# Identity products in TensorE's waits of the first ten slots, and six units of weights moved to later slots

## The chip, the cores and the metric

The kernel runs on one core of a Trainium2 chip. The time is device microseconds of one launch; each kernel is run several times and the median is given. The engines are named as in the profile: TensorE (PE; its weight loads are PEld), VectorE (DVE), ScalarE (ACT), GpSimd (POOL) and SyncE (SP), which issues most of the DMAs. A slot, a word that comes back all through this text, is one turn of the kernel's main loop.

## What is computed

Top-32 attention for 8 batches and 8 heads (576 rows, 64 columns a head), then a bridge to 4608 tokens of 512 features, then a two-layer network with the exact Gelu:

```python
def _attn_ref(q, k, v):
    scores = scale * np.matmul(q, k.transpose(0, 1, 3, 2))
    kth = np.partition(scores, -top_k, axis=-1)[..., -top_k:-top_k + 1]
    scores = np.where(scores >= kth, scores, -1000000000.0)
    attn = np.exp(scores - np.max(scores, axis=-1, keepdims=True))
    attn = attn / (np.sum(attn, axis=-1, keepdims=True) + 1e-09)
    return np.matmul(attn, v).astype(np.float32)
...
    x = np.ascontiguousarray(attn_out.transpose(0, 2, 1, 3)).reshape(B * S, H * D)
    h = x @ w_in
    g = 0.5 * h * (1.0 + erf(h * inv_sqrt2))
    return (g @ w_out).astype(np.float32)
```

q, k and v are float32. The weights w_in (512 x 2048) and w_out (2048 x 512) come as float64, so the kernel turns them into float32 itself.

## The kernel before

An item is 128 query rows of a pair of heads; there are 144 items, 18 for each batch. The main loop runs slots n = 0 to 147, and every engine's instructions stand in the order in which the loop writes them. Slot n does, for different items, all steps of the pipeline:

- TensorE: the scores of item n+2 (t_ps L283 and s_ps L287, or L303 and L314 for the items of the last 64 rows), the product with V of item n-3 where a pair of row blocks is complete (o, L466 or L477; the code calls this `product`), and the transposes of item n-2: the tail (tp_t, L411 or L416), then twice four blocks (tp, L429). In some slots it also transposes parts of q and k of a pair to come (tp_qk, L242; `prep`).
- ScalarE: copies of the scores (L297, L298), two softmax passes of item n-1 (L379 with Prelu, L380 with Exp, once for each head), the copies of the transposed blocks out of PSUM (pt, L412 and L436; qk, L246) and of the product with V into xT (L471, `copy_x`), and Gelu (L529, with its table load).
- VectorE: the top 32 of item n in four rounds (MAX8 L340, MATCH_REPLACE8 L343) for two heads, then the reciprocal of item n-1 (L366).
- GpSimd: thresholds (L355, L358), the denominator (den, L372), and the normalising of item n-1 (L392, two instructions). In slots ahead of some units of weights the normalising is on VectorE instead.

PSUM tiles with the tag tp (transposes, t_ps, o) share two buffers, so a transpose waits until the tile two before it has been copied out.

**The network's pieces.** x @ w_in and g @ w_out are cut into pieces of about 0.9 us on TensorE (`l1_piece`, h_ps L518; `l2_piece`, y_ps L554). `mlp(1)` puts the next piece into the slot, if its tokens are there. The first 256 tokens are complete in slot 10, which the code calls START (2 * NP + 2). Slots 10 and 11 take four pieces each (`left`), later ones eight. What the attention part leaves over is done after the last item.

**Units of weights.** The weights come in 16 units, one a slot, in the order ORDER. A unit takes the low and high words of float64 numbers through one staging tile: `load_weights` issues two DMAs of half a MB in all on SP (L160), `weights_size` is two or three instructions on ScalarE (L175, L177, and L179 where GpSimd doesn't do it), `weights_add` is one addition on GpSimd (L194), preceded by L191 where the unit is "on pool", and a second addition is L206. `SLOT_OF` says which slot a unit is in: before, the places 0 to 14 of ORDER are in slots 1 to 15 and the last is in slot 17. The unit of slot n+1 is sized at the end of slot n and added at the start of slot n+1; the unit of slot n+2 is loaded at the end of slot n. Units in slots up to START get their second addition late in the slot (`ends_late`); units from slot 12 on are "on pool".

The staging tile is a free part of w_out_sb (two halves, taken in turn) for most places of ORDER, and a tile of its own, `words`, with one buffer, for the places 12, 14 and 15, because by then w_out_sb is filling up. A load into a staging tile waits until the unit that was there before has been added.

**Warming up.** Before the loop, nine products of a tile of zeros (L630) run on TensorE while the first DMAs land.

Of the kernel before, what the change touches and what calls it, by code (L numbers as in the profile page):

```python
# [14 lines left out]
def kernel(  # L15
# [19 lines left out]
    nc = tc.nc  # L35
    f32, i32, u32 = mybir.dt.float32, mybir.dt.int32, mybir.dt.uint32
# [5 lines left out]
    P = 128  # L42
# [19 lines left out]
    ps = ctx.enter_context(tc.tile_pool(name="ps", bufs=2, space=bass.MemoryType.PSUM))  # L62
    ctx.enter_context(tc.manual_schedule())

    ident = const.tile([P, P], f32, name="ident")
# [18 lines left out]
    def load(n, pair, queue=None, queue2=None):  # L84
        if pair >= n_pairs:
            return
        queue = queue or nc.sync
        queue2 = queue2 or queue
        b, h0 = pair // NP, 2 * (pair % NP)
        t, src = raw_of(n, pair), sources[n]  # L90
        for e in range(2):
            queue.dma_start(
                out=t[:, 0:NM, e, :], in_=src[b, h0 + e, 0:SM].rearrange("(t p) d -> p t d", p=P)
            )
            queue2.dma_start(out=t[e * TL : (e + 1) * TL, NM, e, :], in_=src[b, h0 + e, SM:S])
# [14 lines left out]
    UNITS = NWI + FT // 2  # L110
# [3 lines left out]
    def weights_of(u):  # L114

        if u < NWI:
            c, r = u // 2 * WS, u % 2 * 2
            return w_in, r, c, w_in_sb[:, r : r + 2, c : c + WS]
        r = 2 * (u - NWI)
        return w_out, r, 0, w_out_sb[:, r : r + 2, :]  # L120


    ORDER = [0, 1, 2, 3, 8, 9, 4, 5, 10, 11, 6, 7, 12, 13, 14, 15]
    FIRST = 1
    START = 2 * NP + 2
    WARM = 9
    words = {}
# [3 lines left out]
    nc.gpsimd.memset(high, EXP0 * 2.0**-21)  # L131


    SLOT_OF = {u: FIRST + i + (i == UNITS - 1) for i, u in enumerate(ORDER)}
    UNIT_IN = {n: u for u, n in SLOT_OF.items()}
    unit_in = UNIT_IN.get

    def load_weights(n, queue=None):

        queue = queue or nc.sync  # L140
        u = unit_in(n)
        if u is None:
            return
        src, r, c, dst = weights_of(u)
        if src.dtype == f32:
            for x in range(2):
                queue.dma_start(
                    out=dst[:, x], in_=src[(r + x) * P : (r + x + 1) * P, c : c + WS]
                )
            return  # L150


        half, i = src.bitcast(u16), ORDER.index(u)
        if i not in (12, 14, 15):
            at = FT // 2 + 4 * (i % 2)
            t = w_out_sb[:, at : at + 4, :].rearrange("p (a b) n -> p a (b n)", a=2)
        else:
            t = stage.tile([P, 2, 2 * WS], f32, tag="words", name="words")
        for a in range(2):
            queue.dma_start(  # L160
                out=t[:, a].bitcast(u16)[:, 0 : 4 * WS - 1],
                in_=half[(r + a) * P : (r + a + 1) * P, 4 * c + 1 : 4 * (c + WS)],
            )
        words[u] = t

    def parts(u):

        t, dst = words[u], weights_of(u)[3].bitcast(i32)
        return t[:, :, 0::2], t.bitcast(mybir.dt.int16)[:, :, 2::4], t[:, :, 1::2].bitcast(i32), dst

    def weights_size(u):
        if u not in words:
            return
        w, first, below, d = parts(u)
        nc.scalar.activation(d, first, func=AF.Relu, bias=low, scale=2.0**19)  # L175

        nc.scalar.activation(below, first, func=AF.Prelu, bias=high, scale=2.0**-21, alpha=2.0**40)  # L177
        if not on_pool(u):
            nc.scalar.activation(w.bitcast(i32), w.bitcast(u32), func=AF.Copy, scale=2.0**-13)  # L179

    def on_pool(u):

        return u in words and SLOT_OF[u] >= START + 2

    made = set()

    def weights_add(u):
        if u in words:
            w, _, below, d = parts(u)
            if on_pool(u):  # L190
                nc.gpsimd.tensor_scalar(  # L191
                    w.bitcast(i32), w.bitcast(u32), 2.0**-13, None, op0=ALU.mult
                )
            nc.gpsimd.tensor_tensor(d, d, below, op=ALU.add)  # L194
            if not ends_late(u):
                weights_end(u)
        made.add(u)

    def ends_late(u):

        return u in words and SLOT_OF[u] <= START

    def weights_end(u):
        if u in words:
            w, _, _, d = parts(u)
            nc.gpsimd.tensor_tensor(d, d, w.bitcast(i32), op=ALU.add)  # L206
# [143 lines left out]
    def threshold(i):  # L350

        if i < 0 or i >= N:
            return
        st = stat_of[i]
        nc.gpsimd.tensor_scalar(  # L355
            st["neg"], st["top"][:, :, 0 :: TOPK - 1], -1.0, None, op0=ALU.mult
        )
        nc.gpsimd.tensor_tensor(  # L358
            st["bias"], st["neg"][:, :, 0], st["neg"][:, :, 1], op=ALU.subtract
        )  # L360

    def inverse(i):
        if i < 0 or i >= N:
            return
        st = stat_of[i]
        nc.vector.reciprocal(st["rden"], st["den"])  # L366

    def add_small(i):
        if i < 0 or i >= N:
            return  # L370
        st = stat_of[i]
        nc.gpsimd.tensor_scalar(st["den"], st["den"], 1e-9, None, op0=ALU.add)  # L372

    def softmax(i, e):

        if i < 0 or i >= N:
            return
        st, s = stat_of[i], row(i, e)
        nc.scalar.activation(s, s, func=AF.Prelu, bias=st["neg"][:, e, 1:2], scale=1.0, alpha=STEEP)  # L379
        nc.scalar.activation(  # L380
            s, s, func=AF.Exp, bias=st["bias"][:, e : e + 1], scale=1.0,
            accum_out=st["den"][:, e : e + 1],
        )
# [56 lines left out]
    def copy_x():  # L440
        while copies:
            copies.pop()()
# [149 lines left out]
    def run_gelus():  # L592
        while waiting:
            gelus(waiting.pop(0))
# [9 lines left out]
    def mlp(n):  # L604
        for _ in range(n):
            if done[0] >= len(pieces) or pieces[done[0]][0] > ready[0] or left[0] == 0:
                return
            pieces[done[0]][1]()
            done[0] += 1
            left[0] -= 1  # L610
            if eager[0]:
                run_gelus()
# [7 lines left out]

    load("k", 1)
    load("q", 1)
    for n in range(2):
        load_weights(FIRST + n)


    idle = raws["v"][0][:, NM].rearrange("p e d -> p (e d)")
    warm = ps.tile([P, 512], f32, tag="l1", name="warm")
    for _ in range(WARM):
        nc.tensor.matmul(warm[:, 0:P], lhsT=idle, rhs=idle, start=True, stop=True)  # L630
    for pair in range(2):
        for piece in transpose_qk(pair, pair == 0):
            piece()
# [17 lines left out]
    for n in range(ahead):  # L651

        left[0] = 4 if n in (START, START + 1) else 8
        eager[0] = n > N
        weights_add(unit_in(n))
        scores(n + 2)
        product = attend(n - 3)
        late = n > START
        if n <= START:

            softmax(n - 1, 0)
        copy_x()
        mlp(1)
        tr = transposes(n - 2)
        if product and n > START and done[0] < len(pieces) and pieces[done[0]][0] > ready[0]:

            for piece in tr[:1]:
                piece()
            tr, ready[0] = tr[1:], n_tok[0]
        if n > START:  # L670
            softmax(n - 1, 0)
        mlp(1)
        if not late:
            softmax(n - 1, 1)
        mlp(1)
        prep = prep_in.pop(n, [])
        if len(prep) > 1 and len(tr) == 3:
            tr, prep = tr[:1] + prep[:1] + tr[1:], prep[1:]
        for piece in tr[:-1]:
            piece()  # L680
            ready[0] = n_tok[0]
            mlp(1)
        ready[0] = n_tok[0]
        if late:
            softmax(n - 1, 1)
        add_small(n - 1)
        if ends_late(unit_in(n)):
            weights_end(unit_in(n))
        for piece in tr[-1:] + prep:
            piece()  # L690
            mlp(1)

        run_gelus()
        mlp(left[0])
        run_gelus()
        if n < N:
            top_k(n, {3: lambda: inverse(n - 1)})
        else:
            inverse(n - 1)
        threshold(n)  # L700
        u = unit_in(n + 1)

        normalise(n - 1, 2 if on_pool(u) else 0)

        weights_size(unit_in(n + 1))
        if n >= FIRST:
            load_weights(n + 2)
        if n <= NP:
            load("v", n)

# [37 lines left out]
```

## Time and profile before

| | |
|---|---|
| median of 5 runs | 1640.95 us (1640.01 to 1642.09) |
| the profiled execution | 1640.01 us, of which its span (first to last instruction) is 1638.2 us |
| mean granted TensorE clock | 0.981 of full speed |
| TensorE busy | 1586.8 us, 97% of the span |
| VectorE busy | 1415.0 us, 86% |
| ScalarE busy | 1185.8 us, 72% |
| GpSimd busy | 663.0 us, 40% |
| chain that ended last | TensorE 92%, ScalarE 5%, all others 1% or less each |

The span differs from the time by what lies before the first and after the last instruction, 1.8 us here. In the page's second part the span is cut into 40 slices of 41 us, and each digit is the busy share of an engine in tenths; PEclk is the TensorE clock that the throttle granted. A list of waits names the waiting instruction, what it waited for by its line, the total in microseconds, how often, and the longest. In a timeline a row is: start, duration, engine, line, operation, output and inputs, how many instructions are merged in it, and in brackets the idle time of the engine just before and what ended it. One f32 product is two records on TensorE, one transpose is one.

A table of windows shows how full the engines are at the start: between 20 and 120 us VectorE is busy for every microsecond, ScalarE for 18.0 to 18.7 of each 20, GpSimd for 14.5 to 18.5 of each 20 and TensorE for 9.8 to 15.0, at a mean granted clock of 0.60 to 0.79. From 140 to 1600 us TensorE is busy at the full clock almost without a gap.

### The profile page before, as it was taken

What the parts mean: (1) busy time and instruction counts of PE and PEld (TensorE: products, weight loads), DVE (VectorE), ACT (ScalarE), POOL (GpSimd) and SP (SyncE); (2) the same over time, 40 slices, a digit from 0 to 9 for tenths busy, and PEclk for the clock granted to TensorE, in tenths of its full rate; (3) what the DMA queues carried; (4) which work ended last, traced back from release to release, by engine and by line L of the source; (5) the groups of instructions that cost most, each with busy time, mean ns of one, the idle gap of its engine ahead of it and who ended that gap; (6) DMA issues with size and microseconds to landing.
All of it is one profiled execution on the core that took longest, in us unless ns stands there. A gap on an engine that the chain in (4) does not pass through costs nothing.

```text
span 1638.2 us, 25030 instructions
## 1 busy us (share of the span) xinstructions
PE 1586.8 (97%) x8818; PEld 1075.2 (66%) x8818; DVE 1415.0 (86%) x3046; ACT 1185.8 (72%) x2133; POOL 663.0 (40%) x759
## 2 busy tenths in 40 slices
PE   5579999999999999999999999999999999999999
PEld 4356676766666666676666667676666666666665
DVE  8999999988898899998989898998889889999800
ACT  6999877777777777777777777777777777777720
POOL 4897533333333333333333333333333333333300
PEclk7779999999999999999999999999999999999999
DMA  6433210011101120001110111001110101000000
GB/s 165 143 110 121 55 43 1 14 33 40 35 1 28 30 51 8 14 16 36 30 28 15 28 30 43 1 14 32 41 36 1 28 16 35 1 14 3 5 13 13
DMA packets 126765, 56.14 MB, mean 34 GB/s; under 512 B 117776, under 2 KB 118064, under 8 KB 126640
## 3 DMA queue, kind: packets, MB, share of 16 engines
q1 hardware_dynamic: 125376, 54.12, 12.3%
q8 instruction: 70, 1.15, 0.3%
q10 hardware_dynamic: 1200, 0.39, 0.1%
q14 instruction: 55, 0.45, 0.1%
q0 software_dynamic: 64, 0.03, 0.0%
HBM read 45.08 MB, written 9.44 MB: 33 GB/s over the span
## 4 chain that ended last, share of the span: by engine, by line
PE 92%; ACT 5%; POOL 1%; issue 1%; DVE 1%; DMA 1%; SPq 0%; ACTq 0%; POOLq 0%; DVEq 0%
PE y_ps L554 30%; PE h_ps L518 30%; PE o L466 9%; PE tp L429 8%; PE s_ps L287 8%; PE tp_qk L242 2%; PE t_ps L283 2%; PE o L477 1%; ACT s L380 1%; PE s_ps L314 1%; PE tp_t L411 1%; ACT s L379 1%; POOL s L392 1%; ACT w_in_sb L175 1%; ACT s L297 1%
## 5 line engine op out<-in xcount | busy, mean ns | idle before, releaser
L340 DVE MAX8 top<-rest 128x8 f32<-128x576 f32 x864 | 609.2, 746 | 0.0
L518 PE MATMUL h_ps<-xT,w_in_sb 128*128 128x256 f32 (+1 forms) x2560 | 553.0, 361 | 0.0
L554 PE MATMUL y_ps<-w_out_sb,g 128*128 128x512 f32 x1152 | 548.9, 599 | 0.0
L392 POOL TENSOR_SCALAR s<-s,rden 128x576 f32<-128x576 f32 x278 | 476.9, 1725 | 0.6 <-DVE rden L366 0.4
L518 PEld LDWEIGHTS h_ps<-xT,w_in_sb 128*128 128x128 f32 x2560 | 428.4, 191 | 61.8 <-issue 16.8
L343 DVE MATCH_REPLACE8 rest<-top,rest 128x576 f32<-128x576 f32 x576 | 423.2, 742 | 0.0
L372 POOL TENSOR_SCALAR den<-den 128x2 f32<-128x2 f32 x144 | 32.0, 222 | 836.2 <-ACT s L380 835.8
L554 PEld LDWEIGHTS y_ps<-w_out_sb,g 128*128 128x128 f32 x1152 | 195.1, 190 | 168.2 <-issue 167.3
L297 ACT ACTIVATE s<-s_ps 128x1024 f32<-128x1024 f32 x127 | 130.5, 1028 | 164.5 <-PE s_ps L287 142.2
L380 ACT ACTIVATE s<-s,bias 128x576 f32<-128x576 f32 x288 | 223.3, 775 | 13.2 <-ACT s L379 0.7
L379 ACT ACTIVATE s<-s,neg 128x576 f32<-128x576 f32 x288 | 224.1, 778 | 0.3 <-POOL neg L355 0.2
L436 ACT COPY pt<-tp 128x512 f32<-128x512 f32 x256 | 147.3, 575 | 101.6 <-PE tp L429 101.6
L429 PEld LDWEIGHTS tp<-ident,s 128*128 128x128 f32 x1152 | 145.6, 144 | 100.8 <-issue 58.9
L343 DVE MATCH_REPLACE8 rest<-top,s 128x576 f32<-128x576 f32 x288 | 211.7, 743 | 0.0
L340 DVE MAX8 top<-s 128x8 f32<-128x576 f32 x288 | 201.7, 742 | 1.4 <-ACT s L293 1.4
L429 PE MATMUL tp<-ident,s 128*128 128x128 f32 x1152 | 178.0, 278 | 14.1 <-ACT pt L412 11.6
L466 PE MATMUL o<-pt,raw_v 128*64 128x256 f32 x1280 | 155.8, 391 | 0.0
L287 PE MATMUL s_ps<-qk 64*128 64x256 f32 x1024 | 151.5, 416 | 0.8 <-ACT s L295 0.8
L366 DVE RECIPROCAL rden<-den 128x2 f32<-128x2 f32 x144 | 23.1, 160 | 137.7 <-POOL den L372 137.4
L466 PEld LDWEIGHTS o<-pt,raw_v 128*64 128x64 f32 x1280 | 87.8, 139 | 66.6 <-issue 22.8
L287 PEld LDWEIGHTS s_ps<-qk 64*128 64x128 f32 x1024 | 91.3, 193 | 23.4 <-issue 1.3
L529 ACT ACTIVATE g<-h_ps 128x512 f32<-128x512 f32 x144 | 78.6, 595 | 37.8 <-PE h_ps L518 37.1
(71 smaller groups left out, 1075.2 us busy)
## 6 DMA issues: line engine op xcount, KB each, us to landing
raw_q<-in_q_dram SPq DMA_DIRECT2D x64, 128.0 KB, 2.4
raw_v<-in_v_dram SPq DMA_DIRECT2D x64, 128.0 KB, 2.5
w_out_sb<-in_moe_w_in_dram SPq DMA_DIRECT2D x16, 511.8 KB, 4.9
raw_k<-in_k_dram SPq DMA_DIRECT2D x62, 128.0 KB, 2.5
out_dram<-y SPq DMA_DIRECT2D x31, 256.0 KB, 2.2
w_out_sb<-in_moe_w_out_dram SPq DMA_DIRECT2D x10, 511.8 KB, 3.9
words<-in_moe_w_out_dram SPq DMA_DIRECT2D x6, 511.8 KB, 4.5
out_dram<-y SPq DMA_DIRECT2D x9, 128.0 KB, 2.3
```

The costliest lines, as they stand in the source:

```text
L287: nc.tensor.matmul(s_ps[:, e, c * 256 : (c + 1) * 256], lhsT=lhsT[rows, :], rhs=qk[rows, KT + c * 256 : KT + (c + 1) * 256], start=True, s ...
L297: nc.scalar.activation(spread(s, S + TL, SM), s_ps, func=AF.Copy, scale=scale)
L340: nc.vector.max(st["top"][:, e, 8 * r : 8 * r + 8], cur[e])
L343: nc.vector.match_replace(rest[:, e], st["top"][:, e, 8 * r : 8 * r + 8], cur[e], LOWEST)
L379: nc.scalar.activation(s, s, func=AF.Prelu, bias=st["neg"][:, e, 1:2], scale=1.0, alpha=STEEP)
L380: nc.scalar.activation(s, s, func=AF.Exp, bias=st["bias"][:, e : e + 1], scale=1.0, accum_out=st["den"][:, e : e + 1],)
L392: (nc.vector if e >= 2 - on_dve else nc.gpsimd).tensor_scalar(s, s, st["rden"][:, e : e + 1], None, op0=ALU.mult)
L429: nc.tensor.transpose(tp[:, j * P : (j + 1) * P], s[:, first + j * P : first + (j + 1) * P], ident)
L436: nc.scalar.copy(out=dst, in_=tp.rearrange("p (j n) -> p j n", j=NM))
L466: nc.tensor.matmul(o[e * D : (e + 1) * D, 0:n], lhsT=vt[:, j, e, :], rhs=pt[:, e * NM + j if j < NM else 2 * NM, :], start=(j == 0), stop= ...
L518: nc.tensor.matmul(h_tile(u)[:, i, :], lhsT=w_in_sb[:, ko, f * P : (f + 1) * P], rhs=xT[:, ko, c0 : c0 + n], start=(ko == 0), stop=(ko == ...
L554: nc.tensor.matmul(y_of[sub], lhsT=g_of[u][:, i, sub * P : (sub + 1) * P], rhs=w_out_sb[:, f, :], start=(f == 0), stop=(f == FT - 1),)
```

## The change

It has two parts.

First, products of the identity matrix. The warm-up loop becomes a function, `keep_busy(count, m)`, which still runs the nine products of zeros at the start. In slots 0 to 9 it is called again with the identity: after the second softmax pass has been written and ahead of the transposes (4 products in slot 0 and in slots with a product with V, 14 in the others), between the tail's transpose and the first four blocks in the slots with a product with V (5), and at the end of slot 1 (8). From slot 5 on the first two numbers are doubled. In all there are 183 such products: 4, 22, 14, 14, 9, 28, 18, 28, 18, 28 in slots 0 to 9. Their result is never read.

Second, the slots of the units. The places 0 to 9 of ORDER stay in slots 1 to 10; the six others go to slots 13 to 18 in place of 11 to 15 and 17. Slots 11 and 12 have no unit, slots 16 and 18 get one. The last unit (slot 18) is handled apart (`waits`): it is loaded at the end of slot 17 and not of slot 16, and sized and added within slot 18, behind `copy_x`. The unit at place 2 of ORDER (slot 3) is staged in `words`. "On pool" now means every unit after START, six in place of five.

```diff
-    FIRST = 1
...
-    SLOT_OF = {u: FIRST + i + (i == UNITS - 1) for i, u in enumerate(ORDER)}
+    SLOT_OF = dict(zip(ORDER, [*range(1, START + 1), *range(START + 3, START + 9)]))
...
-        if i not in (12, 14, 15):
+        if i not in (2, 12, 14, 15):
...
-        return u in words and SLOT_OF[u] >= START + 2
+        return u in words and SLOT_OF[u] > START
+
+    def waits(u):
+
+        return u == ORDER[-1]
...
-    warm = ps.tile([P, 512], f32, tag="l1", name="warm")
-    for _ in range(WARM):
-        nc.tensor.matmul(warm[:, 0:P], lhsT=idle, rhs=idle, start=True, stop=True)
+    def keep_busy(count, m):
+        warm = ps.tile([P, 512], f32, tag="l1", name="warm")
+        for _ in range(count):
+            nc.tensor.matmul(warm[:, 0:P], lhsT=m, rhs=m, start=True, stop=True)
+
+    keep_busy(WARM, idle)
...
-        weights_add(unit_in(n))
+        if not waits(unit_in(n)):
+            weights_add(unit_in(n))
...
         copy_x()
+        if waits(unit_in(n)):
+            weights_size(unit_in(n))
+            weights_add(unit_in(n))
...
+        if n < START:
+
+            keep_busy((4 if product or n == 0 else 14) * (1 if n < 5 else 2), ident)
...
             piece()
+            if n < START and product and piece is tr[0]:
+                keep_busy(5 if n < 5 else 10, ident)
...
+        if n == 1:
+            keep_busy(8, ident)
...
-        weights_size(unit_in(n + 1))
-        if n >= FIRST:
-            load_weights(n + 2)
+        if not waits(unit_in(n + 1)):
+            weights_size(unit_in(n + 1))
+        for m in (n + 1, n + 2):
+
+            if m > 2 and waits(unit_in(m)) == (m == n + 1):
+                load_weights(m)
```

More of the change, by code (lines that the diff above doesn't have):

```diff
@@ L622 @@
     load("q", 1)
-    for n in range(2):
-        load_weights(FIRST + n)
+    for n in range(1, 3):
+        load_weights(n)
     idle = raws["v"][0][:, NM].rearrange("p e d -> p (e d)")
-    warm = ps.tile([P, 512], f32, tag="l1", name="warm")
-    for _ in range(WARM):
-        nc.tensor.matmul(warm[:, 0:P], lhsT=idle, rhs=idle, start=True, stop=True)
+    def keep_busy(count, m):
[3 more added lines that the diff above has]
+    keep_busy(WARM, idle)
     for pair in range(2):
```

## The prediction

> **What bounds the kernel now.** I read the slices of the page first, then TensorE's waits by stretch, then two-microsecond windows around the turn, then the timeline of ScalarE and TensorE there.
>
> ```profile
> PE   5579999999999999999999999999999999999999
> DVE  8999999988898899998989898998889889999800
> ACT  6999877777777777777777777777777777777720
> PEclk7779999999999999999999999999999999999999
> ```
>
> Each digit is 41 us. In the first three slices VectorE is full, TensorE is half busy and its granted clock is low; after that TensorE is full to the end. So the end is (the moment from which TensorE never waits) + (the work it then has). VectorE takes 9.70 us a slot (its reciprocals L366 stand at 88.05, 97.75, 107.45 and 117.15) and has no idle time in the ten slots before the turn. Nothing that happens on TensorE before slot 10 is worth anything unless it moves that turn.
>
> ```profile
> PE tp_t L411 <- POOL s L392: 3.7, 1, 3.7
> PE tp L429 <- ACT pt L412: 2.4, 2, 1.8
> PE t_ps L283 <- ACT pt L436: 1.6, 2, 1.4
> ...
> PE tp L429 <- ACT pt L412: 0.8, 1, 0.8
> PE tp_t L416 <- POOL s L392: 0.7, 1, 0.7
> ...
> PE tp_t L416 <- POOL s L392: 0.7, 1, 0.7
> ```
>
> TensorE's waits (us, times, longest) in 100 to 135, 135 to 200 and 200 to 1570 us. All that can still be won behind the turn is here: from 114 us on 0.64 + 1.39 (slot 11), 0.79 (slot 12), 0.72 (slot 18) and 0.7 near the end.
>
> ```profile
> 104.00:106.00 2.00, 0.26 (x2) 0.00 (x0) 2.00 (x6) 1.97 (x7) 1.30 (x2) 0.50 0.00 0
> ...
> 110.00:112.00 2.00, 2.00 (x12) 0.85 (x10) 2.00 (x5) 2.00 (x3) 2.00 (x2) 0.50 0.86 256
> ...
> 114.00:116.00 2.00, 2.00 (x14) 1.80 (x13) 2.00 (x6) 1.97 (x7) 0.92 (x1) 1.00 0.02 4
> ```
>
> Columns: PE, PEld, DVE, ACT, POOL busy, granted clock, DMA. TensorE enters slot 10 at half clock and has the full one from about 113. But ScalarE is full too:
>
> ```profile
> 107.21 0.59 ACT L436 COPY pt<-tp 128x512 f32<-128x512 f32 x1 [0.72 <-PE tp L429]
> ...
> 116.94 0.59 ACT L436 COPY pt<-tp 128x512 f32<-128x512 f32 x1 [0.26 <-PE tp L429]
> ...
> 127.72 0.49 PE L283 MATMUL t_ps<-qk 128*128 128x128 f32 x2 [1.39 <-ACT pt L436]
> ...
> 137.43 0.66 PE L429 MATMUL tp<-ident,s 128*128 128x128 f32 x4 [0.79 <-ACT pt L412]
> ```
>
> ScalarE waits for TensorE once a slot, for the second four transposes: 0.72 us where the clock is halved (four take 1.11), 0.26 where it is full (0.66). TensorE's waits behind the turn are waits for ScalarE's queue, in which 3.5 us of weights (L175, L177, L179) stand in slot 11 and 2.4 in slot 12.
>
> **Part 1, the identity products (183 of them).** Slots 0 to 4 get 4, 22, 14, 14, 9; slots 5 to 9 get 28, 18, 28, 18, 28. Price of one: no row shows it. Lower end: four transposes at full clock, each with its own weight load, pass in 0.44 us (135.18 to the next at 135.62), 0.11 a record; a product has two records, so 0.22. The nine products of zeros at the start agree: 18 records in 4.2 us, 0.23 a record, at a halved clock (the transposes at 5.11 still take 1.08 for four, at 6.98 only 0.66). Upper end: one 128-column product t_ps keeps TensorE from 118.90 to 119.22, 0.32. I take 0.22, a stream of equal records.
>
> [...]
>
> Do they hold the clock? The waits after which it falls are 3.66 (slot 9) and 4.15 to 4.50 (slots 5, 7); across 1.34 and 1.07 (slot 6) it stays at 1.0. Slot 9: scores end at 99.2, 28 x 0.22 = 6.2 fill up to 105.4, so the wait of 3.66 is gone. They write to the l1 buffers, which nothing reads before slot 10.
>
> What it is worth: not the shorter o products (3.43 to 2.38), because behind them TensorE waits in slot 10 for ScalarE: the second transposes at 116.24 wait for a copy behind the softmax, which ends at 115.94 on a queue that was full. So the gain is ScalarE's lead. Waits of 0.72 stand in slots 2, 3, 5, 7 and 9; each becomes 0.26: 5 x 0.46 = 2.3. Two caps. Slot 8: its first four transposes come after ten products, which come after the tail, which needs VectorE's end of slot 7 (88.05) + threshold 0.5 + two L392 of 1.72 = 92.0; + 0.1 + 10 x 0.22 + 0.6 = 94.9, against the copy at 96.24 now: a lead of 1.3 at most. Slot 9: from t_ps (97.72) 0.32 + 1.06 + 6.16 + 0.11 + 0.6 = 8.25 against 8.19 now (copy at 105.91): -0.1, then + 0.46. Lead at the turn: 1.3 - 0.1 + 0.46 = 1.7. Its ends: 0 if a product costs 0.235, 2.3 if the caps don't bind.
>
> **Part 2, six units later.** Slots 11 and 12 lose theirs, 16 and 18 gain one; 13, 14, 15 and 17 keep one. The unit that was in slot 11 had three ScalarE instructions, now two; GpSimd does the third (L191, 3.13), so GpSimd gains 3.1 and ScalarE loses 1.1 us, both beside a full TensorE. Normalising on VectorE (two of 0.52) leaves slot 11 and enters the end of slot 15, before a reciprocal that waits 2.01 for den: covered.
>
> Slot 11: without weights ScalarE takes the scores when they are there, 120.35 instead of 122.20, but then waits for TensorE: its first four transposes end at 124.55 as before. Then copy 0.5, softmax 1.6, copy 0.5: t_ps of slot 12 at 127.27, not 127.72: 0.45 won, and 1.4 us of waiting stay. Slot 12: scores copied 2.9 us after t_ps, not 5.1; the tail's copy is 2 us earlier and the 0.79 goes.
>
> Slot 16 is the price. There ScalarE starts with a table load and Gelu, now followed by L175 and L177 (2.43 at 185.59 to 188.02). Gelu ends at 175.5; weights to 177.95; scores, xT, first softmax pass, table, Exp: the tail's copy ends at 182.5, and the transposes due at 181.87 need its buffer: 0.63 lost. In slot 14, the same shape, Gelu ran 0.9 earlier against t_ps and TensorE didn't wait. Behind it nothing more is late: the last copy of the slot ends at 186.2, t_ps is due at 186.5.
>
> Slot 18: the unit is sized behind copy_x in its own slot, so its wait for the DMA stands ahead of the tail's copies and the softmax on ScalarE. GpSimd is done with the words buffer in slot 17 at 194.05 + 0.63; issue and 4.5 us to landing (3.6 to 6.8 seen for this tile) give 199.8, ScalarE comes there at 199.9; two activations to 202.4, tail copies to 203.0, and the transposes need them at 203.7. Taken at 0; at 6.8 it costs 1.5. SP's queue behind this load holds V loads that now issue at 209.95. The last unit isn't in words when slot 17 normalises, so that stays on GpSimd, and so does the 0.72. GpSimd then ends the unit at 208.4; its first use is slot 19's fifth piece, after 213.
>
> The words buffer for slot 3's unit takes a wait from SP's queue that was 0.1 us (30.92, issued right behind K at 30.30): nothing.
>
> **Sum.** 1.7 + 0.45 + 0.79 - 0.63 = 2.3 us. The profiled execution had a span of 1638.2 in 1640.01; it becomes 1635.9 in 1637.7. The median of the runs is 0.94 above it: 1638.6. Own range 1637.0 to 1640.2 (lead 0.5 to 2.5, slot 16 at 0 to 1).
>
> **Rivals.**
> - All waits go (chance 0.20). TensorE runs on from slot 10: 1.7 + 0.64 + 1.39 + 0.79 + 0.72 = 5.2, so 1635.7 (1634.8 to 1637.2). For it: ScalarE loses 6 us of work in slots 11 and 12. Against: in slot 11 the softmax can't start before TensorE's transposes.
> - The lead is given back (0.17). At 0.235 a product slots 5 to 9 lose 120 x 0.015 = 1.8: 1640.4 (1639.5 to 1643, with slot 18 late). For it: 8.25 against 8.19 in slot 9.
> - Slower: the products are too long (0.13). At 0.32 each odd slot's chain grows by 28 x 0.10 = 2.8 three times, each even one by 1.8 less its 0.5 of slack twice: 11.0 later, less five waits of 0.46, less 0.6 from part 2: 8.1, so 1649. VectorE would not notice (the scores copied at 101.48 are wanted at 117.2), but TensorE and ScalarE would enter slot 10 late and never catch up. Decides from 0.265 (5.6 us lost over 120 products). Against: the transposes' 0.11 a record.
>
> Forecast 0.50. A difference under 0.2% (3.3 us) can't be told from none here: faster means under 1637.7. That is 0.12 of the forecast and the first rival, 0.32; slower 0.13; the rest 0.55. The range 1635.2 to 1642.0 leaves out the slow rival and the edges of two others, 0.18.
>
> **What would show it.** Right: granted clock 1.0 in every window from 40 to 120 us; ScalarE's wait before L436 0.26 in slots 5, 7 and 9; products 0.22 apart; t_ps of slot 12 near 125.6; a wait near 0.6 in slot 16 and none in slot 12. Wrong: products 0.25 apart or more, first transposes of slots 5, 7, 9 later than now, a wait for DMA on ScalarE in slot 18, or VectorE idle before slot 11.

## The result, and the profile after

The changed kernel takes 1638.75 us (median of 25 runs, 1637.57 to 1644.4); the kernel before, run on the same chips, 1640.93 (45 runs, 1639.82 to 1642.7). The ratio is 0.9989, 95% interval 0.9983 to 0.9994. The forecast was 1638.6 us. The gain can be measured, but at 0.11% to 0.13% it lies below the 0.2% from which the prediction calls a kernel faster.

The profiled execution took 1637.79 us, with a span of 1636.0. Lines of the kernel that stood at L283 or behind it are four higher now: t_ps is L287, s_ps L291, the transposes tp L433, the tail tp_t L415 or L420, the normalising L396. The slices of the page and the chain that ended last:

```profile
PE   7999999999999999999999999999999999999999
DVE  8999999988898899998989899998889889999800
ACT  6989877777777777777777777777777777777720
PEclk9999999999999999999999999999999999999999
...
PE 91%; DVE 5%; ACT 2%; POOL 1%; issue 0%; SPq 0%; DMA 0%; DVEq 0%; POOLq 0%; ACTq 0%
```

TensorE is now full, and at nine tenths of its clock or more, in the second and third slices too, from 41 to 123 us. The work that fills them has no use of its own: TensorE's busy time rose by 26.3 us (1586.8 to 1613.1), the time fell by 2. The chain tells more: before, ScalarE had 5% of it, now VectorE has. The early part of this chain now runs through the engine that was full there all along. TensorE's waits in 100 to 135 and 135 to 200 us. From 200 us on there is none, and there was none before either: the 0.7 that the prediction reads as "near the end" is slot 18's wait once more, as its transpose runs from 199.94 us across the border at 200. It stands in none of the prediction's sums.

```profile
PE t_ps L287 <- ACT pt L440: 1.8, 2, 1.4
PE tp_t L415 <- POOL s L396: 1.3, 1, 1.3
PE tp L433 <- ACT pt L416: 0.4, 2, 0.2
...
PE tp_t L420 <- POOL s L396: 0.7, 1, 0.7
PE tp L433 <- ACT pt L416: 0.5, 1, 0.5
```

The 3.7 of slot 9 and the 0.8 of slot 12 are gone. The 1.4 of slot 11 and the 0.7 of slot 18 stand as forecast. A 1.3 in slot 10 is new (TensorE is early there and waits until GpSimd has normalised the tail), and so is the 0.5 of slot 16. The windows around the turn, and three earlier ones:

```profile
38.00:40.00 2.00, 1.95 (x8) 1.41 (x10) 2.00 (x5) 1.93 (x3) 2.00 (x2) 0.67 0.03 8
40.00:42.00 2.00, 2.00 (x10) 1.27 (x7) 2.00 (x6) 1.99 (x2) 1.92 (x3) 0.50 0.51 111
50.00:52.00 2.00, 2.00 (x12) 0.94 (x10) 2.00 (x6) 2.00 (x3) 2.00 (x2) 0.50 0.58 133
104.00:106.00 2.00, 1.66 (x13) 1.11 (x11) 2.00 (x6) 1.74 (x5) 1.16 (x3) 1.00 0.00 0
110.00:112.00 2.00, 0.66 (x5) 0.51 (x4) 2.00 (x5) 1.91 (x4) 2.00 (x2) 1.00 0.00 0
```

At 104 and 110 us, where the clock was 0.50, it is 1.00. But at 40 and 50 us it is still 0.50 (0.86 on average from 40 to 60 us): the sign "1.0 in every window from 40 to 120 us" did not come for slots 3 and 4, and the experiments come back to that. TensorE's timeline:

```profile
92.02 0.33 PE L415 MATMUL tp_t<-ident,s 128*128 128x128 f32 x1 [0.67 <-POOL s L396]
92.19 2.40 PE L636 MATMUL warm<-ident 128*128 128x128 f32 x20
94.42 1.04 PE L433 MATMUL tp<-ident,s 128*128 128x128 f32 x8
...
97.67 6.52 PE L636 MATMUL warm<-ident 128*128 128x128 f32 x56
104.02 0.27 PE L415 MATMUL tp_t<-ident,s 128*128 128x128 f32 x1
...
125.77 0.49 PE L287 MATMUL t_ps<-qk 128*128 128x128 f32 x2 [1.39 <-ACT pt L440]
...
179.56 0.66 PE L433 MATMUL tp<-ident,s 128*128 128x128 f32 x4 [0.49 <-ACT pt L416]
```

Slot 9's 28 products pass from 97.67 to the tail at 104.02, 0.227 us each. ScalarE's side of it:

```profile
95.06 1.07 ACT L440 COPY pt<-tp 128x512 f32<-128x512 f32 x2 [0.82 <-PE tp L433]
...
105.62 0.59 ACT L440 COPY pt<-tp 128x512 f32<-128x512 f32 x1 [0.26 <-PE tp L433]
...
115.43 0.59 ACT L440 COPY pt<-tp 128x512 f32<-128x512 f32 x1 [0.26 <-PE tp L433]
```

The second copies of slots 9 and 10 (105.62, 115.43) wait 0.26, where the clock is full, not 0.72; in slots 5 to 8 the two copies stand in one row, with no such wait between them. Slot 8's first copy waits for TensorE at 95.06: the cap that the prediction put at 94.9.

Where the 2.2 us of span came from can be read off the starts of t_ps, the first product of a slot, before minus after: 1.59 in slot 10, 1.50 in slot 11, 1.95 in slot 12, 2.96 in slots 13 to 16, 2.25 from slot 17 on, and nothing more happens to the end. So the gain at the turn (the point from which TensorE hardly waits any more) is 1.50, slot 11 brings 0.45, slot 12 brings 1.01, slot 16 takes 0.71. Of the 1.50, 0.17 is no work of the change: VectorE itself had started that much earlier in this execution (its reciprocal of slot 9 at 107.28, before at 107.45).

### The profile page after: what moved, and what is told of

Read it like the earlier page. It is cut to its first block, busy times and chain, and to the rows that moved or that the text cites. A ratio compares the mean times of both kernels' runs of the same rounds, so it can differ in the third digit from the quotient of the medians.

```text
span 1636.0 us, 25758 instructions
## 1 busy us (share of the span) xinstructions
PE 1613.1 (99%) x9184; PEld 1106.8 (68%) x9184; DVE 1414.8 (86%) x3046; ACT 1186.1 (73%) x2132; POOL 665.9 (41%) x760
## 4 chain that ended last, share of the span: by engine, by line
PE 91%; DVE 5%; ACT 2%; POOL 1%; issue 0%; SPq 0%; DMA 0%; DVEq 0%; POOLq 0%; ACTq 0%
PE h_ps L522 30%; PE y_ps L558 30%; PE o L470 8%; PE s_ps L291 7%; PE tp L433 7%; DVE top L344 3%; DVE rest L347 2%; PE tp_qk L246 2%; PE t_ps L287 2%; PE o L481 1%; PE tp_t L415 1%; PE s_ps L318 1%; POOL s L396 1%; ACT s L384 0%; ACT s L383 0%
## 5 line engine op out<-in xcount | busy, mean ns | idle before, releaser
L396 POOL TENSOR_SCALAR s<-s,rden 128x576 f32<-128x576 f32 x278 | 476.8, 1725 | 0.6 <-DVE rden L370 0.4
L433 PEld LDWEIGHTS tp<-ident,s 128*128 128x128 f32 x1152 | 142.5, 141 | 88.9 <-issue 58.9
L433 PE MATMUL tp<-ident,s 128*128 128x128 f32 x1152 | 172.8, 273 | 3.7 <-ACT pt L416 3.3
L291 PE MATMUL s_ps<-qk 64*128 64x256 f32 x1024 | 147.1, 406 | 0.8 <-ACT s L299 0.8
L291 PEld LDWEIGHTS s_ps<-qk 64*128 64x128 f32 x1024 | 89.1, 188 | 22.4 <-ACT s L299 1.0
```

The source lines that it names most:

```text
L291: nc.tensor.matmul(s_ps[:, e, c * 256 : (c + 1) * 256], lhsT=lhsT[rows, :], rhs=qk[rows, KT + c * 256 : KT + (c + 1) * 256], start=True, s ...
L396: (nc.vector if e >= 2 - on_dve else nc.gpsimd).tensor_scalar(s, s, st["rden"][:, e : e + 1], None, op0=ALU.mult)
L433: nc.tensor.transpose(tp[:, j * P : (j + 1) * P], s[:, first + j * P : first + (j + 1) * P], ident)
```

## The experiments

Times are medians with the lowest and highest run, and the ratio is to the kernel before, timed beside them on the same chip (medians 1640.64 to 1641.22). Every trace is that of one execution. Diffs are against the changed kernel where nothing else is said.

### Each part alone

The products without the moved units: the slots, the staging and the order of the units as before. This diff is against the kernel before; `keep_busy` itself is left out of it.

```diff
+        if n < START:
+
+            keep_busy((4 if product or n == 0 else 14) * (1 if n < 5 else 2), ident)
...
+            if n < START and product and piece is tr[0]:
+                keep_busy(5 if n < 5 else 10, ident)
...
+        if n == 1:
+            keep_busy(8, ident)
```

> The identity products alone, with the units in their old slots. Theory (the terms add): ScalarE's lead of 1.5 us at the turn is kept through slots 11 and 12, whose waits of 0.64, 1.39 and 0.79 stay, and slot 16 has no wait: 1640.95 - 1.5 = 1639.4. Rival (the lead is worth something only because slots 11 and 12 are free of weights): the weights of slot 11 swallow it and the time is 1640.9.

The moved units without the products:

```diff
-        if n < START:
-
-            keep_busy((4 if product or n == 0 else 14) * (1 if n < 5 else 2), ident)
...
-            if n < START and product and piece is tr[0]:
-                keep_busy(5 if n < 5 else 10, ident)
...
-        if n == 1:
-            keep_busy(8, ident)
```

> The moved units alone, without any identity product. Theory: 0.45 won in slot 11, 0.8 to 1.0 in slot 12, 0.5 lost in slot 16, so about 0.95 in all: 1640.0, with ScalarE's waits of 0.72 still in slots 5, 7 and 9 and the clock at 0.5 there. Rival (the later units stall slots 16 and 18 for more than they free): 1641.5 or more.

Measured: the products alone 1639.24 (1638.67 to 1639.79, 11 runs; ratio 0.9990, 0.9981 to 0.9999), the slots alone 1640.31 (1639.75 to 1641.56, 11 runs; 0.9998, 0.9989 to 1.0007). Against 1640.83 that is 1.6 and 0.5, 2.1 together, where the whole change brings 2.2: the parts add up. The second can't be told from zero by its interval, but its trace can tell: t_ps takes 8.37 us from slot 11 to slot 12 as in the changed kernel (8.82 before), 12.01 over slot 12 (13.02 before) and 13.19 over slot 16 (12.46 before), 0.7 in all. The span of that execution is only 0.2 us shorter than before, because it came to slot 11 0.53 late (119.43 against 118.90), as it had to slot 10 (108.37 against 107.85). Its mean clock from 20 to 40 us was 0.50, before 0.60; that the half microsecond comes from there is the author's estimate and not shown.

The trace of the products alone also shows what a short wait really costs. TensorE in slot 12, first the products alone, where the 0.8 is still there, then the changed kernel:

```profile
134.29 1.03 PE L518 MATMUL h_ps<-xT,w_in_sb 128*128 128x256 f32 x4
136.10 0.65 PE L429 MATMUL tp<-ident,s 128*128 128x128 f32 x4 [0.78 <-ACT pt L412]
136.60 1.03 PE L518 MATMUL h_ps<-xT,w_in_sb 128*128 128x256 f32 x4
```

```profile
133.66 1.03 PE L522 MATMUL h_ps<-xT,w_in_sb 128*128 128x256 f32 x4
134.53 0.60 PE L433 MATMUL tp<-ident,s 128*128 128x128 f32 x4
134.97 1.03 PE L522 MATMUL h_ps<-xT,w_in_sb 128*128 128x256 f32 x4
```

From one h_ps to the next (134.29 to 136.60, 133.66 to 134.97) it is 2.31 against 1.31, so the wait in brackets, 0.78, costs 1.00. In an unbroken stream h_ps takes 0.87 to the next row, though its own row says 1.03: the ends overlap. A wait takes this overlap (0.16) as well, and the transposes behind it take 0.50 to the next row and not 0.44. That makes 0.22 more than the bracket says.

### The unit that moved into slot 16

```diff
-    SLOT_OF = dict(zip(ORDER, [*range(1, START + 1), *range(START + 3, START + 9)]))
+    SLOT_OF = dict(zip(ORDER, [*range(1, START + 1), *range(START + 2, START + 6), START + 7, START + 8]))
```

The six units are in slots 12, 13, 14, 15, 17 and 18, none in slot 16.

> The change with the six units in slots 12, 13, 14, 15, 17 and 18, so none in slot 16. Theory: the 0.49 of slot 16 comes back, but slot 12's wait for the second transposes returns with 1.0, as Gelu, its table loads and the weights stand there together too: 0.5 slower than the change, 1639.3. Rival (slot 12's old wait came from slot 11's weights alone, so slot 12 has room): 0.49 faster, 1638.3.

Measured 1639.54 (1637.81 to 1643.68, 11 runs; 0.9992, 0.9984 to 1.0001). The wait of slot 16 is gone, and the 0.8 of slot 12 is back: a unit in slot 12 makes ScalarE late there again, as in the kernel before. Slot 16 is the cheaper of the two by 0.3 (1.01 against 0.71), in the direction of the medians, which differ by less than these runs spread, so the times alone decide nothing here. The rest of the 0.9 by which this execution's span is longer than the changed kernel's is a smaller lead at slot 10, which the account of the lead below takes up.

### The products that are too many, or not needed

Eight more in each of slots 5, 7 and 9:

```diff
-            keep_busy((4 if product or n == 0 else 14) * (1 if n < 5 else 2), ident)
+            keep_busy((4 if product or n == 0 else 14) * (1 if n < 5 else 2)
+                      + (8 if n >= 5 and not product else 0), ident)
```

> The change with 36 products in slots 5, 7 and 9 instead of 28. Theory (TensorE's chain from t_ps to the first transposes is as long as ScalarE's slot, so each product more is paid): 8 x 0.22 = 1.76 more in each odd slot, so 1.3 of lead lost in each net of the 0.46 won; lead -3.0 instead of 1.5, time 4.5 above the change: 1643.2. Rival (VectorE and GpSimd set the pace of these slots and the products only fill waits): 1638.8, as the change.

Measured 1643.7 (1643.1 to 1644.92, 10 runs; 1.0017, 1.0008 to 1.0026), 5.0 above the changed kernel; its theory said 4.5. TensorE in slot 9:

```profile
101.43 8.30 PE L636 MATMUL warm<-ident 128*128 128x128 f32 x72
109.57 0.27 PE L415 MATMUL tp_t<-ident,s 128*128 128x128 f32 x1
...
111.53 0.49 PE L287 MATMUL t_ps<-qk 128*128 128x128 f32 x2
```

The tail passes 5.55 us later than in the changed kernel (104.02). Of this, 1.06 was there when slot 5's products began (59.99 against 58.93); then each eight products add 1.79, 0.22 each, in slots 5, 7 and 9 alike, and slots 6 and 8 give back 0.31 and 0.58. So nothing of them is hidden in their own slots: 28 is the whole of the room, as the prediction said (8.25 of work against 8.19), and as slot 9 of the changed kernel shows as well, where ScalarE takes the first transposes (104.13 to 104.73) at 104.78 without a wait. This is the mechanism of its slower rival, with that rival's 0.5 of slack in the even slots. Only VectorE did notice: in this trace it is busy for 19.84, 19.24 and 18.34 of each 20 us from 60 to 120, in the changed kernel for all of them.

The count not doubled in slots 5 to 9:

```diff
-            keep_busy((4 if product or n == 0 else 14) * (1 if n < 5 else 2), ident)
+            keep_busy((4 if product or n == 0 else 14), ident)
...
-                keep_busy(5 if n < 5 else 10, ident)
+                keep_busy(5, ident)
```

> The change with the numbers of slots 0 to 4 in slots 5 to 9 too: 14 in odd slots, 4 and 5 in even ones. Theory: the gap that is left in odd slots is 2.4 to 2.8 us, less than the 3.66 across which the clock fell before, so the clock holds; the cap of slot 8 (products behind the tail) is lifted by 1.1 and slot 9's chain is short, so the lead becomes 2.2 and the time 0.7 below the change: 1638.05. Rival (the clock falls in such gaps): waits of 0.72 back in slots 5, 7, 9, lead 0.5 at most, 1639.8.

Measured 1638.82 (1637.34 to 1639.51, 11 runs; 0.9986, 0.9977 to 0.9995), between its theory and its rival. The theory's clock did not hold: it fell with half the products, to 0.91, 0.91 and 0.70 in 60 to 80, 80 to 100 and 100 to 110 us, and slot 9's second copy waited 0.72 again. t_ps of slot 10 starts at 106.59, 0.33 later than in the changed kernel, yet the median is the changed kernel's within its spread: the doubling is worth a few tenths at most, and these runs don't say more.

None in slots 0 to 4:

```diff
-        if n < START:
+        if 5 <= n < START:
...
-            if n < START and product and piece is tr[0]:
+            if 5 <= n < START and product and piece is tr[0]:
...
-        if n == 1:
-            keep_busy(8, ident)
```

> The change without the 63 products of slots 0 to 4. Theory: the lead comes from slots 5, 7 and 9 alone, 3 x 0.46 less 0.1 = 1.3 instead of the 1.5 of the change, so the time is 0.2 above the change's 1638.75: 1638.95. Rival (the early products hold the clock for slot 5; without them its 28 products run at half clock, 12 us instead of 6): lead gone, 1642 or more.

Measured 1639.3 (11 runs; 0.9995, 0.9986 to 1.0004), in two heaps: six runs from 1638.65 to 1639.3, five from 1640.93 to 1641.69. The median is the top of the lower heap, which lies where the theory put the time; the upper heap lies a little below the rival's 1642. But the rival's mechanism is not what happened: in the profiled execution, which is of the upper heap (1641.5), slot 5's 28 products passed at full clock, from 61.41 us on (1.00 in 60 to 80 us). TensorE's row and VectorE's, from the two timelines:

```profile
52.98 4.24 PE L470 MATMUL o<-pt,raw_v 128*64 128x256 f32 x20
```

```profile
59.58 0.17 DVE L370 RECIPROCAL rden<-den 128x2 f32<-128x2 f32 x1 [0.59 <-POOL den L376]
```

The product with V of slot 4 falls into a stretch at half clock (4.24; 3.38 before), and VectorE, which has no wait in these slots in the changed kernel, waits 0.59 us for a denominator. Its reciprocals were 0.14 behind the changed kernel's until then (49.21 against 49.07) and are 0.8 behind from there on (69.30 against 68.47, 108.11 against 107.28). TensorE's lead is gone too: t_ps of slot 10 comes 0.31 after VectorE's reciprocal (before 0.40 after it, in the changed kernel 1.02 ahead of it). Together that is 2.1 us at slot 11. The other 1.64 of this execution's loss is a lower clock in slot 12 (scores in 1.98 and product with V in 3.17, at full clock 1.13 and 2.38), far behind slots 0 to 4; all_filled shows the same fall below, and what brings it on stays open.

### The lead, and what caps it

The lead is how much earlier than before ScalarE, and with it t_ps of slot 10, comes to the turn. The prediction's first cap on it is slot 8: first the tail, then ten products, then the transposes. Four of the ten moved ahead of the tail:

```diff
-            keep_busy((4 if product or n == 0 else 14) * (1 if n < 5 else 2), ident)
+            keep_busy((4 if product or n == 0 else 14) * (1 if n < 5 else 2)
+                      + (4 if n >= 5 and product else 0), ident)
...
-                keep_busy(5 if n < 5 else 10, ident)
+                keep_busy(5 if n < 5 else 6, ident)
```

> The change with 4 of the 10 products behind the tail in slots 6 and 8 moved ahead of the tail (12 and 6 instead of 8 and 10). Theory (the cap of slot 8 is what holds the lead at 1.5; ScalarE waits 0.82 there and TensorE 0.67 ahead of the tail): lead 0.6 to 0.7 larger, 1638.1. Rival (the next limit, GpSimd's normalising ahead of slot 10's tail, where TensorE waits 1.34 already, takes it): 1638.75.

Measured 1639.9 (1637.44 to 1641.36, 11 runs; 0.9992, 0.9983 to 1.0001). The median is beyond even the rival's 1638.75, but the runs lie in two heaps again, and in the profiled execution the clock was low by the second transposes of slot 3 (four took 1.12 us at 47.05, 0.65 in the changed kernel): t_ps of slot 4 came at 49.70 (48.57 in the changed kernel), and TensorE came to slot 8 late, with the tail at 93.01 waiting for nothing. So this execution didn't try the cap; the early clock had to be steadied first. TensorE's waits ahead of that place are those of slots 2 and 3. The next kernel fills them in part, and the one behind it repeats the split on top:

```diff
-            keep_busy((4 if product or n == 0 else 14) * (1 if n < 5 else 2), ident)
+            keep_busy((4 if product or n == 0 else 18 if n == 2 else 14) * (1 if n < 5 else 2), ident)
...
-            if n < START and product and piece is tr[0]:
+            if n < START and (product or n in (2, 3)) and piece is tr[0]:
```

> The changed kernel, with 18 products in place of 14 in slot 2 and 5 more behind the tail's transpose in slots 2 and 3, where its trace shows TensorE waiting 1.09, 1.16 and 1.28 us and the clock at half in the scores of slots 3 and 4 (s_ps 2.08 at 39.06 and 49.01). My theory: those waits let the clock go, and what it does afterwards differs from execution to execution, which is most of the spread of the changed kernel (1637.6 to 1644.4): with them filled, scores of 1.14 in slots 3 and 4, the product with V of slot 4 in 2.4, t_ps of slot 10 still near 106.3 (what holds it is the tail and the products of slot 8), a spread of some 1.5 us, and a median of 1637.9. Rival: the early slots are behind VectorE, and the clock there costs the end nothing: the median stays at 1638.75 with the same spread, or rises if the products in slot 3 now come too late for ScalarE.

> The kernel before in this call (early5) with 12 products ahead of the tail and 6 behind it in slots 6 and 8, in place of 8 and 10. If the tail and the ten products behind it hold the lead in slot 8, as the prediction has it, the second copies of slot 8 come 0.7 to 0.9 earlier (near 94.2, with the clock steady), t_ps of slot 10 near 105.5, and the median is 0.6 below early5's: 1637.3. Rival: what then binds is slot 9's own chain (1.06 + 28 products) or the tail behind 12 products: t_ps of slot 10 within 0.2 of early5's, the same time.

Measured: early5 1638.19 (1637.41 to 1639.98, 11 runs; 0.9987, 0.9978 to 0.9996); early5_split 1637.52 (1637.12 to 1638.97, 11 runs; 0.9981, 0.9972 to 0.9990). Slot 4 in early5, then in the changed kernel:

```profile
49.45 1.13 PE L291 MATMUL s_ps<-qk 64*128 64x256 f32 x8
50.51 2.38 PE L470 MATMUL o<-pt,raw_v 128*64 128x256 f32 x20
```

```profile
49.01 2.08 PE L291 MATMUL s_ps<-qk 64*128 64x256 f32 x8
51.02 3.00 PE L470 MATMUL o<-pt,raw_v 128*64 128x256 f32 x20
```

In early5's trace the filled waits do hold the clock: 1.00 in 20 to 40 and in 40 to 60 us, and a mean over the whole kernel of 0.999 or 1.0 in ten of the 11 runs (0.992 to 0.999 in the changed kernel's). The highest of the 11 runs is 1639.98 now, with no outlier, though the spread of 1.5 us that was expected came out as 2.6. And the cap is real. Slot 8's tail and first copies in early5_split:

```profile
92.60 0.33 PE L415 MATMUL tp_t<-ident,s 128*128 128x128 f32 x1 [0.66 <-POOL s L396]
94.74 1.07 ACT L440 COPY pt<-tp 128x512 f32<-128x512 f32 x2 [0.72 <-PE tp L433]
```

Against the tail's start, slot 8's first copy is at +3.04 in the changed kernel and in early5, and at +2.14 with six products behind the tail: 0.90 less, four products of 0.227. Against VectorE's reciprocal near 107.5, t_ps of slot 10 starts 0.40 after it in the kernel before, 1.02 and 0.99 ahead of it in the changed kernel and early5, and 1.91 ahead in early5_split: a lead won of 1.4 (0.40 + 1.02) with ten products behind the tail and of 2.3 (0.40 + 1.91) with six, the number that the prediction gave "if the caps don't bind". That it is the same number is chance: slot 8's first copy still waits 0.72 for TensorE, so this cap still binds, only later. The median fell by 0.67 (0.6 expected), with six runs from 1637.12 to 1637.52 and five from 1638.3 to 1638.97, and the two intervals overlap; the trace shows the gain more clearly than the times. This version beats the kernel before by 0.19%, and its median lies 1.2 below the changed kernel's, on another chip.

### Where the rest of the spread is

In early5_split's profiled execution, one of its longer ones (1638.97), TensorE in slot 10:

```profile
112.01 0.33 PE L415 MATMUL tp_t<-ident,s 128*128 128x128 f32 x1 [2.19 <-POOL s L396]
...
113.08 1.06 PE L433 MATMUL tp<-ident,s 128*128 128x128 f32 x4
```

The greater the lead, the longer this wait, since GpSimd's tail comes 4.15 us after VectorE's reciprocal here, as it does 4.18 after it in the changed kernel and 4.21 in early5, with TensorE waiting each time. Behind it the clock was 0.75, 0.50 and 0.90 in the three windows from 112 to 118, and from t_ps of slot 10 to that of slot 11 it took 12.67 us, 11.14 in the changed kernel: 1.5 lost. So seven products were put into this wait, in both versions:

```diff
+        if n == START:
+            keep_busy(7, ident)
         prep = prep_in.pop(n, [])
```

> early5_split with seven more products in slot 10, between the product with V and the tail's transpose. In its trace TensorE waits 2.19 us there for GpSimd (the tail is normalised 4.15 us after VectorE's reciprocal, whatever TensorE does), the clock falls to half right behind it, the four transposes then take twice as long, ScalarE's second copy waits 1.76 in place of 0.26, and t_ps of slot 11 comes at 118.62 although t_ps of slot 10 was 0.31 earlier than in the changed kernel. My theory: this wait is the other place where the clock goes in some executions; with it filled the clock is 1.0 in 100 to 120, the second copy waits 0.26, t_ps of slot 11 is at 117.1 to 117.3, and no run is above 1637.9: a median near 1637.2, a spread under 1 us. Rival: the products come too late for the tail or take the buffer that the first pieces want, or the turn is set by the tail itself: t_ps of slot 11 no earlier than 117.4, median 1637.5 or above, and runs above 1638.5 stay.

> The changed kernel with these seven products in slot 10 alone. If both places (the waits of slots 2 and 3, and this one) take part in its spread, the median falls by less than half a microsecond, to 1638.3 to 1638.7, and runs above 1640 stay, as the early waits are open still. If slot 10 is the only place, the runs stay within 1.5 us and the median is near early5_split's, 1637.5. If it is no part of it, 1638.75 and the same spread.

Measured: all_filled (on early5_split) 1638.62 (1637.43 to 1640.43, 11 runs; 0.9985, 0.9977 to 0.9994), fill10 (on the changed kernel) 1638.52 (1638.29 to 1644.53, 11 runs; 0.9990, 0.9981 to 0.9999). Of all_filled's theory the slot itself came true: the clock is 1.00 from 110 to 120 us, the second copy waits 0.26, and t_ps of slot 11 follows that of slot 10 by 11.12 us, not 12.67. What fell is that no run would be above 1637.9. Two slots on, in slot 12:

```profile
126.60 0.49 PE L287 MATMUL t_ps<-qk 128*128 128x128 f32 x2 [1.39 <-ACT pt L440]
127.02 1.42 PE L291 MATMUL s_ps<-qk 64*128 64x256 f32 x8
128.37 3.73 PE L470 MATMUL o<-pt,raw_v 128*64 128x256 f32 x20
```

The 1.39 us that t_ps waits here in early5 and fill10 too is followed, this time, by a lower clock (0.77 in 125 to 130 us): 3.73 for a product with V that takes 2.38 in those two behind the very same wait. With the scores' 1.42 (1.13 there) slot 12 takes 13.65 us and not 12.01: 1.64 us are lost, as much as no_early loses in the same place. VectorE had also started late, its first MAX8 of a full tile at 11.48 us, against 10.37 in the changed kernel; slot 11's tail waits 0.42 for GpSimd, and from t_ps of slot 11 to that of slot 12 it takes 9.01 us and not 8.37. Whether filling slot 10 makes the fall in slot 12 likelier, these runs don't tell. fill10 went as its first case said, a median 0.2 lower and runs above 1640 still there, but a 0.2 in medians of this spread can't be told from its third case, no part at all.

### More pieces in slot 11's wait

The 1.39 could be work: two more pieces of the network at the end of slot 11.

```diff
+        if n == START + 1:
+            left[0] += 2
         mlp(left[0])
```

> The change with two more pieces of the network at the end of slot 11 (6 instead of 4), into the 1.39 us for which TensorE waits there ahead of slot 12's t_ps. Theory (from here TensorE's work sets the end, and that wait is the largest left): 1.39 less at the end, 1637.4. Rival (scores of slot 12 come 0.34 later and ScalarE passes it on as waits in slot 12, or the pieces move Gelu to a worse place): gain 0.5 or less, 1638.3 to 1638.8.

Measured 1654.13 (1652.86 to 1655.12, 4 runs; 1.0080, 1.0066 to 1.0093). Both theories were wrong, by 15 us and more; the rival named a worse place for Gelu, but as a smaller gain and not as a loss. TensorE's waits in 100 to 200 us, its timeline, and ScalarE's:

```profile
PE h_ps L522 <- ACT g L533: 9.8, 3, 3.8
```

```profile
128.75 3.46 PE L522 MATMUL h_ps<-xT,w_in_sb 128*128 128x256 f32 x8 [3.77 <-ACT g L533]
132.04 0.38 PE L287 MATMUL t_ps<-qk 128*128 128x128 f32 x2
```

```profile
126.80 1.28 ACT L533 ACT_TABLE_LOAD   x1
128.09 1.08 ACT L533 ACTIVATE g<-h_ps 128x512 f32<-128x512 f32 x2
```

The extra piece needs a PSUM buffer that Gelu must free, and Gelu stands behind the softmax and a table load of 1.28 us. A wait of 1.39 for one engine became 3.77 for the same engine further down its queue, and two more such waits follow. These 9.8 us are most of the loss. The clock has a part in the rest (0.91 in 120 to 140 us): behind the 3.77 two pieces take 3.46 (at full clock 1.89), and behind the next such wait, 2.57, t_ps takes 0.70 (0.45). What is left was not followed.

## Why the prediction was right, step by step

**What bounds.** Right: the end is the turn plus the work behind it. TensorE's shorter waits and shorter products of slots 5 to 9 counted only as lead at slot 10, and from slot 17 on the two kernels run in parallel.

**Price of a product.** 0.227 measured against 0.22 taken. The row of four transposes, 0.11 a record, was the right guide. The upper end, the 0.32 that one t_ps takes, does not hold for these products; the trace decides. The prediction reads a halved clock under the nine products of zeros from the length of the transposes behind them (1.08 us for four at 5.11, 0.66 at 6.98); the windows from 0 to 8 us of that trace show a granted clock of 1.00, so the halving there is not shown.

**Lead at the turn.** 1.7 forecast, 1.50 measured, of which 0.17 was VectorE's earlier start: mis-sized by 0.2 to 0.4. The cap of slot 8 was right in kind (95.06 against 94.9) and is shown by early5_split. Most of the missing part is in its size: the tail came 4.14 us after VectorE's reciprocal (87.88 to 92.02) and not 3.95, and the ten products took 2.40 to the transposes and not 2.30, so slot 8's first copy won 1.18 and not 1.3 (1.01 without VectorE's start). Slot 9's -0.1 came out as -0.05 and its 0.46 as 0.46.

The clock of slots 3 and 4, forecast at 1.0 and measured at 0.50, is a step that failed without harm to this execution. The prediction let the clock fall only behind waits of 3.66 us and more and had it "stay at 1.0" across the 1.34 and 1.07 of slot 6. In that very trace it falls behind them, in the scores of slot 7 (0.65 in 78 to 80 us; scores at full clock take 1.13):

```profile
78.25 1.76 PE L287 MATMUL s_ps<-qk 64*128 64x256 f32 x8
```

With the early clock mended, early5's t_ps of slot 10 stands where the changed kernel's does against VectorE, so the lead of 1.42 doesn't miss it. But it matters where the clock falls. In skip16 and fill2, whose first ten slots are the changed kernel's, the mean clock was 1.00 from 20 to 40 and 0.83 from 40 to 60 us, and the lead at slot 10 was 0.75 and 0.82. In the changed kernel, where it fell earlier (from 38 to 42 us and again around 50), the two means were 0.97 and 0.86, as in p1_products, and the lead was 1.42 and 1.40. So in these four traces some 0.6 us go with the place of the early fall.

**Slot 11.** 0.45 forecast, 0.45 measured; t_ps at 125.77 for "near 125.6", with its 1.4 of waiting left, as forecast. **Slot 12.** 0.79 forecast, 1.01 measured. **Slot 16.** 0.63 lost forecast, a wait of 0.49 measured, but 0.71 lost. In both a wait cost 0.22 more than its bracket; a sum made of brackets is here too small by that for each wait that goes or comes. In slot 12 this is the whole difference; in slot 16 the bracket itself had been taken 0.14 too large, which hides most of it.

**Slot 18.** 0, and 0: ScalarE's L175 starts at 197.05 directly behind copy_x, without a wait for the DMA, and the 0.72 for GpSimd stays.

**Sum.** 2.3 forecast; 2.25 at slot 17; 2.2 in the span and in the medians. The path and its terms were right, but so close a sum is partly luck: a lead 0.2 too large (0.37 without VectorE's start) stands against 0.22 too little in slot 12.

**Rivals.** That all waits go did not happen: the 1.39 and the 0.72 are there. That the lead is given back did not: products at 0.227 were just short enough. That they are too long did not, and odd36 shows how close its edge is.

**Signs.** One of the signs of being wrong did come: the first transposes of slots 5 and 9 start later than before (65.39 against 64.96, 104.13 against 103.20). It was a badly chosen sign. By the prediction's own working for slot 9 they end 8.25 us after t_ps, where ScalarE comes to take them, while before they were done early and lay waiting; that they start later costs nothing until ScalarE has to wait.

## What to carry to other kernels

Where an engine must be kept at its clock through idle stretches, count how much of each stretch is room: in this kernel the filler was free up to that, and from there every product cost its full 0.22 us. Place filler ahead of a late operand and not behind it; four products moved to the other side of the tail were worth 0.9 us of lead in the trace and 0.7 in the medians, a third of what the change brings. And read a wait that goes as its bracket plus the overlap of the rows around it, here 0.78 + 0.22.

## What the runs showed of the hardware that was not expected

In these traces a wait of the same length let the clock go in one execution and not in another. Behind the 1.39 us ahead of slot 12 the clock was full in the changed kernel, early5 and fill10, and fell in all_filled (0.77 in 125 to 130 us) and no_early (0.91 in 120 to 140 us, the scores of slot 12 in 1.98 and not 1.13); behind 1.34 us in slot 10 of the changed kernel it was full, behind the 2.19 of early5_split halved; behind the 1.16 us of slot 2 it was halved in the changed kernel (scores of slot 3 in 2.08 us) and full in split (1.13). What decides between the two is shown by no run here. Each such fall cost 1.5 to 1.6 us where it hit the path (slot 10 of early5_split, slot 12 of all_filled and no_early).

The changed kernel, with a mean clock of 0.992 to 0.999, spreads more (1637.57 to 1644.4) than the kernel before, whose mean clock was lower in every run (0.979 to 0.984) and whose times are 1639.82 to 1642.7. That such falls are the cause is likely but shown only for the traces above. The mean clock alone doesn't give the time: the changed kernel's three runs at 0.999 took 1637.7 to 1638.4 and its runs at 0.994 and 0.992 took 1640.2 and 1644.4, but those at 0.997 took anything from 1637.57 to 1639.81. What happens in the runs near 1644, of which fill10 and skip16 have one each (0.992 too), stays open: none of them was profiled.
